# Moving the first quarter of w_out to a float32 load on SyncE, and balancing the first convolution over four tiles

## The chip, the cores and the metric

The kernel runs on one core of one Trainium2 chip. The metric is the device time of one execution in microseconds (us). Before the change it was 718.6 us, the median of five executions (718.43 to 719.05). Where a ratio of two kernels is given, it is the mean time of the one kernel's runs over that of the other's of the same rounds, so it is not quite the ratio of the medians quoted beside it.

## The reference

A causal convolution over seven positions, with one set of softmax weights for each of eight heads, feeds a two-layer network with an ELU between the layers:

```python
w = softmax(weight)                         # 8 heads x 7 taps
out[b, s, h, :] = sum_k w[h, k] * x_pad[b, s + k, h, :]
h = out.reshape(32768, 192) @ w_in          # 192 x 2048
g = where(h > 0, h, exp(min(h, 0)) - 1)
return g @ w_out                            # 2048 x 192
```

## The kernel before

The 32768 tokens are worked off in 32 super-blocks of 1024, and each of them in 16 blocks of 128 hidden columns. For each block and each half of the tokens (a "unit"; there are 1024), TensorE makes h, ACT takes the exponential into E, GpSimd clamps E, VectorE forms gT from E and h, and TensorE multiplies gT by w_out. ACT also reads out the convolution of later super-blocks (csb) and the finished results (osb). A small planner in the kernel fixes the order of the matmuls from estimated landing times (LANDS). All engines work strictly in order.

The first super-block is special. Its convolution runs on x transposed by TensorE, with seven diagonal "tap" matrices, in 64x64 tiles; three of the taps of its first third are made by VectorE:

```python
rows_of = [
    [(0, tap, 0, GS, 0) for tap in range(KSIZE - ON_DVE)]          # ON_DVE = 3
    + [(2, t, GS // 2 * c, GS // 2 * (c + 1), 2 + c) for c in range(2) for t in range(KSIZE)],
    [(1, tap, 0, GS, 1) for tap in range(KSIZE)],
]
```

From the second super-block on, the convolution (the "main conv") uses a band matrix Tm. SyncE makes it by writing wband to DRAM and reading it back in a skewed pattern:

```python
sy.dma_start(xh[:, :], ...)
W(s_tap, 3)
sy.dma_start(<conv_band in DRAM>, wband)       # 288 KB
W(s_band, 16)
sy.dma_start(Tm, band[:, P - 1 : ...])         # 256 KB
... xl; then, when w_in has landed, w_in's upper half by a copy within SBUF
```

GpSimd issues the loads that cast to 16 bits, all before its first clamp:

```python
load_w_in(0); load_w_in(1)                     # six loads
load_w_out(0)                                  # blocks 0 to 3
load_x(1, 0); load_x(1, 1)
load_w_out(1); load_w_out(2)                   # blocks 4 to 7, 8 to 15
load_x(2, 0); load_x(2, 1)
for i, (n, u) in enumerate(units):
    for to_load in x_before.get(i, ()):        # load_x(3, 0) before unit 0
        load_x(*to_load)
    W(s_exp, i + 1)
    g.tensor_scalar(out=E, in0=E, ... ALU.min ... ALU.max)
```

ACT copies the first two parts of w_in into the upper partitions after it has read out the first convolution (att); VectorE copies two more.

## Time and profile before

| | before |
|---|---|
| time, median of 5 | 718.6 us |
| span of the profiled run | 716.9 us |
| TensorE busy; weight loads | 99%; 95% |
| first exponential on ACT | 11.39 us |
| first clamp on GpSimd | 12.88 us |
| first gT on VectorE | 13.54 us |
| Tm landed; first csb on ACT | 18.37; 19.99 us |
| last gT | 706.05 us |

The rows from the first exponential down are start times in the trace, from the start of the span; landings are those of the DMA's semaphore. The steady stretch: 32 units take 21.74 us.

### The profile page before, as it was taken

The page shows a single profiled execution, that of the slowest core. Times are in us where ns is not written, and L with a number is a line of the kernel's source. Part 1 is how long each engine was busy: PE and PEld are TensorE (multiplying, and loading weights), DVE is VectorE, ACT ScalarE, POOL GpSimd, SP SyncE. Part 2 cuts the span into 40 slices and gives each one's busy share as a digit, 9 for nine tenths or more (in the row PEclk, how much of TensorE's full clock was granted, in tenths as well). Part 3 has the DMA queues.
Part 4 walks back from the last instruction along what each step waited for, and adds up shares of the span by engine and source line. Part 5 has one row for each costly group of instructions (what it writes and reads, how often), then busy time and mean ns, then how long its engine had stood idle before and what let it go on. Part 6 is the DMA issues. An engine that isn't in the chain of part 4 may idle for free.

```text
span 716.9 us, 27665 instructions
## 1 busy us (share of the span) xinstructions
PE 711.2 (99%) x11875; PEld 681.8 (95%) x11875; DVE 641.2 (89%) x1048; ACT 677.7 (95%) x1290; POOL 665.1 (93%) x1112
## 2 busy tenths in 40 slices
PE   8999999999999999999999999999999999999998
PEld 4689999999999999999999999999999999999998
DVE  7999889998898998899998989988989988999994
ACT  6999999999999999999999999999999999999994
POOL 9999999999999999999999999999999999999893
PEclk9999999999999999999999999999999999999999
DMA  9635334564443553444553344544445534444212
GB/s 185 97 72 95 66 73 78 94 86 75 79 80 74 94 90 64 78 86 79 87 91 70 72 76 95 87 73 77 84 73 90 94 63 76 88 81 83 62 44 69
DMA packets 132303, 58.80 MB, mean 82 GB/s; under 512 B 98374, under 2 KB 131412, under 8 KB 132180
## 3 DMA queue, kind: packets, MB, share of 16 engines
q0 software_dynamic: 43504, 16.77, 22.4%
q1 hardware_dynamic: 88388, 39.37, 22.2%
q8 instruction: 93, 1.52, 0.9%
q10 hardware_dynamic: 288, 0.88, 0.4%
q14 instruction: 30, 0.25, 0.1%
HBM read 34.63 MB, written 25.46 MB: 84 GB/s over the span
## 4 chain that ended last, share of the span: by engine, by line
PE 96%; POOL 2%; ACT 1%; DVE 0%; issue 0%; DVEq 0%; POOLq 0%
PE H L1052 54%; PE H L1029 37%; PE H L1004 4%; POOL xg L627 1%; ACT E L756 1%; POOL E L710 1%; POOL w_in L647 0%; POOL w_out L658 0%; DVE gT L866 0%; ACT csb L752 0%; POOL owner L675 0%; DVE osb L857 0%; POOL block L685 0%; POOL ident L664 0%; POOL ones L662 0%
## 5 line engine op out<-in xcount | busy, mean ns | idle before, releaser
L866 DVE SCALAR_TENSOR_TENSOR gT<-E,H 128x512 f16<-128x512 f32 x1024 | 631.9, 682 | 63.0 <-POOL E L710 59.0
L1029 PE MATMUL H<-att,w_in 64*128 64x512 bf16 x3072 | 679.9, 376 | 1.3 <-DVE gT L866 1.0
L1052 PE MATMUL H<-w_out,gT 64*128 64x192 f16 x8192 | 680.7, 243 | 0.1
L710 POOL TENSOR_SCALAR E<-E 128x512 f32<-128x512 f32 x1024 | 604.3, 613 | 39.9 <-ACT E L756 33.3
L1052 PEld LDWEIGHTS H<-w_out,gT 64*128 64x128 f16 x8192 | 606.8, 94 | 17.4 <-PE H L1052 1.5
L756 ACT ACTIVATE E<-H 128x512 f32<-128x512 f32 x1024 | 584.9, 600 | 23.9 <-PE H L1029 0.5
L1029 PEld LDWEIGHTS H<-att,w_in 64*128 64x128 bf16 x3072 | 274.9, 93 | 8.1 <-DVE gT L866 3.1
L1004 PE MATMUL H<-xg,Tm 64*128 64x240 bf16 x496 | 90.9, 263 | 0.0
L752 ACT ACTIVATE csb<-H 112x480 bf16<-112x480 f32 x124 | 70.8, 571 | 0.5 <-PE H L1004 0.3
L763 ACT ACTIVATE osb<-H 128x384 f32<-128x384 f32 (+1 forms) x129 | 61.9, 482 | 6.9 <-PE H L1052 6.8
L627 POOL DMA_DIRECT2D xg<-in_x_dram x62 | 54.8, 886 | 0.2 <-issue 0.2
L1004 PEld LDWEIGHTS H<-xg,Tm 64*128 64x128 bf16 x496 | 42.5, 94 | 1.2 <-DVE gT L866 0.3
L857 DVE COPY osb<-H 128x192 f32<-128x192 f32 x1 | 0.4, 357 | 7.3 <-PE H L1052 7.3
L903 PE MATMUL H<-const-bfloat16-1.0 128*128 128x512 bf16 x12 | 4.6, 547 | 0.8 <-PEq L1119 0.8
L903 PEld LDWEIGHTS H<-const-bfloat16-1.0 128*128 128x128 bf16 x12 | 1.4, 126 | 2.7 <-issue 2.5
L647 POOL DMA_DIRECT2D w_in<-in_moe_w_in_dram x6 | 3.6, 611 | 0.0
L732 ACT ACTIVATE xb<-xs 128x512 bf16<-128x512 f32 x2 | 1.1, 622 | 2.4 <-DMA xs<-in_x_dram 2.4
L978 PE MATMUL H<-xT,taps 64*64 64x256 bf16 (+1 forms) x50 | 2.6, 317 | 0.0
L658 POOL DMA_DIRECT2D w_out<-in_moe_w_out_dram x3 | 2.5, 850 | 0.0
L978 PEld LDWEIGHTS H<-xT,taps 64*64 64x64 bf16 x50 | 2.0, 106 | 0.5 <-issue 0.2
L725 ACT ACT_TABLE_LOAD x1 | 1.3, 1283 | 1.2 <-PEq L1119 1.2
L936 PEld LDWEIGHTS H<-ident,xb 64*64 64x64 bf16 x48 | 1.2, 126 | 1.1 <-ACT xb L732 1.1
(44 smaller groups left out, 20.2 us busy)
## 6 DMA issues: line engine op xcount, KB each, us to landing
out_dram<-osb SPq DMA_DIRECT2D x126, 192.0 KB, 2.8
xg<-in_x_dram POOLq DMA_DIRECT2D x61, 240.0 KB, 4.6
xs<-in_x_dram ACTq DMA_DIRECT2D x1, 768.0 KB, 4.6
w_in<-in_moe_w_in_dram POOLq DMA_DIRECT2D x6, 128.0 KB, 4.6
att<-csb SPq DMA_TRANSPOSE x31, 3.9
w_out<-in_moe_w_out_dram POOLq DMA_DIRECT2D x2, 192.0 KB, 8.0
w_out<-in_moe_w_out_dram POOLq DMA_DIRECT2D x1, 384.0 KB, 11.9
w_in<-w_in SPq DMA_DIRECT2D x1, 336.0 KB, 6.7
```

Of the source, the lines that this page charges most:

```text
L627: g.dma_start(xg[0:rows, b, 2 * w0 + gr : 2 * w1 : 2, :], src).then_inc(s_x[b][gr], 16)
L647: g.dma_start(w_in[0:HP, j, c0:c1], bass.AP(tensor=moe_w_in.tensor, offset=8 * j * FF + c0, ap=[[CPH * FF, HEADS], [FF, 8], [1, c1 - c0]], ...
L710: g.tensor_scalar(out=E[:, i % NE, :], in0=E[:, i % NE, :], scalar1=1.0, scalar2=0.0, op0=ALU.min, op1=ALU.max,).then_inc(s_clp)
L752: a.activation(*conv_evac(W, m), ACT.Copy).then_inc(s_ce)
L756: a.activation(E[:, i % NE, :], H[:, bank_of[item], :], ACT.Exp).then_inc(s_exp)
L763: a.activation(*out_evac(W, *item[1:]), ACT.Copy).then_inc(s_oev[item[2]])
L866: v.scalar_tensor_tensor(out=gT[:, s % NG3, q, u, :], in0=E[:, i % NE, :], scalar=1.0, in1=H[:, bank_of[item], :], op0=ALU.subtract, op1=A ...
L903: pe.matmul(H[:, bank, :], nc.const_aps.tensor(1.0, (P, P), BF16), nc.const_aps.tensor(1.0, (P, GS), BF16), start=True, stop=True,)
L978: ins = pe.matmul(H[to, bank_of["d", j] + (j == 2 and c0 > 0), c0:c1], taps[rows, tap, rows], xT[rows, j, HALO - PAD + tap + c0 : HALO - P ...
L1004: ins = pe.matmul(H[:, bank_of["c", m], 256 * q : 256 * q + UC], Tm[rows, h, :], xg[rows, s % NXB, :, CPH * h : CPH * (h + 1)].rearrange(" ...
L1029: ins = pe.matmul(H[:, bank_of[item[:3]], :], w_in[HP * r : HP * (r + 1), j, FC * q : FC * (q + 1)], att[HP * r : HP * (r + 1), s % 2, j, ...
L1052: ins = pe.matmul(acc_of(k, g)[:, D * kb : D * (kb + 1)], gT[HP * rt : HP * (rt + 1), t % NG3, q, g, t0 : t0 + P], w_out[HP * rt : HP * (r ...
```

## The change

Its intent: relieve GpSimd of an issue and a half before its first clamp, and finish the first convolution sooner. The first quarter of w_out (blocks 0 to 3) comes as float32 on SyncE, and VectorE casts it. The other three quarters come in one load. The first convolution is spread over all four tiles, with two taps on VectorE in place of three. ACT's w_in copies move ahead of its att copies. (The diff is cut: the new buffer wo, its semaphore, a memory bank, the planner's lookup and TensorE's wait for the cast are left out.)

```diff
-WOUT = (0, 4, 8, 16)
+WOUT = (0, 4, 16)
-ON_DVE = 3
+ON_DVE = 2
+SPLIT = 352
-LANDS = {... "w_out": (3900.0, 8400.0, 11000.0)}
+LANDS = {... "w_out": (2200.0, 9700.0)}
@@ GpSimd
-            load_w_out(0)
             for gr in range(2):
                 load_x(1, gr)
             load_w_out(1)
-            load_w_out(2)
@@ ACT
+            W(s_w[0], 48)
+            for k in range(2):
+                upper_half(*UPPER[k])
             W(s_first[1], 1)
             a.activation(*first_att(1, 0, GS), ACT.Copy).then_inc(s_fa)
             W(s_first[2], 1)
-            a.activation(*first_att(2, 0, GS // 2), ACT.Copy).then_inc(s_fa)
-            W(s_w[0], 48)
-            for k in range(2):
-                upper_half(*UPPER[k])
+            a.activation(*first_att(2, 0, SPLIT), ACT.Copy).then_inc(s_fa)
@@ VectorE
             (two copies of 64 partitions read the crossed part of att)
+            W(s_w[3], 16)
+            v.tensor_copy(w_out[:, 0 : WOUT[1], :], wo[:, :, :]).then_inc(s_wo)
@@ TensorE
-                        + [(2, t, GS // 2 * c, GS // 2 * (c + 1), 2 + c) for c in range(2) for t in range(KSIZE)],
-                        [(1, tap, 0, GS, 1) for tap in range(KSIZE)],
+                        + [(2, tap, 0, SPLIT, 2) for tap in range(KSIZE)],
+                        [(1, tap, 0, GS, 1) for tap in range(KSIZE)]
+                        + [(2, tap, SPLIT, GS, 3) for tap in range(KSIZE)],
@@ SyncE, between xh and conv_band
+            W(s_xs, 16)
+            sy.dma_start(
+                wo[:, :, :],
+                moe_w_out.rearrange("(q p) d -> p q d", p=FC)[:, 0 : WOUT[1], :],
+            ).then_inc(s_w[3], 16)
```

More of the change, by code (lines that the diff above doesn't have):

```diff
@@ L60 @@
 EARLY_O = (4, 8)
-LANDS = {"x": {1: 7200.0, 2: 14200.0}, "w_in": 10200.0, "w_out": (3900.0, 8400.0, 11000.0)}
+LANDS = {"x": {1: 7200.0, 2: 14200.0}, "w_in": 10200.0, "w_out": (2200.0, 9700.0)}
 DONE_PE, TO_ACT, TO_POOL, TO_DVE, TO_PE = 165.0, 40.0, 85.0, 35.0, 60.0
@@ L266, in o_ready @@
             if k < 2:
-                t = max(t, LANDS["w_out"][next(i for i in range(3) if q1 <= WOUT[i + 1])])
+                t = max(t, LANDS["w_out"][next(i for i in range(2) if q1 <= WOUT[i + 1])])
             if visit == 0:
@@ L456, in bass_lightweight_conv__then__act_elu_kernel @@
         scr = sbuf("scr", [P, 2], FP32)
+        wo = sbuf("wo", [P, WOUT[1], D], FP32)
         H = psum("H", [P, NBANK, GS])
@@ L470, in bass_lightweight_conv__then__act_elu_kernel @@
         s_wb = sema("s_wb")
+        s_wo = sema("s_wo")
         s_xz = sema("s_xz")
@@ L535, in bass_lightweight_conv__then__act_elu_kernel @@
             ("d", 1): (3, 0),
-            ("d", 2): (4, 4),
+            ("d", 2): (4, 5),
         }
@@ L850, in _vector @@
             W(s_first[3], 1)
-            v.tensor_copy(*first_att(2, GS // 2, GS)).then_inc(s_fd)
+            to, at = first_att(2, SPLIT, GS)
+            for g in range(2):
+                v.tensor_copy(
+                    to[HP * g : HP * (g + 1), :], at[HP * (1 - g) : HP * (2 - g), :]
+                ).then_inc(s_fd)
             W(s_w[0], 48)
@@ L976, in _tensor @@
                         for r in range(2):
-                            rows, to = half_of(r), half_of(r ^ (j == 1))
+                            rows, to = half_of(r), half_of(r ^ (which % 2))
                             ins = pe.matmul(
@@ L1048, in _tensor @@
                         W(s_turn[g], turns[k, g])
-                    W(s_w[2 + next(k for k in range(1, 4) if q < WOUT[k])], 16)
+                    if q < WOUT[1]:
+                        W(s_wo, 1)
+                    else:
+                        W(s_w[4], 16)
                     W(s_tt, tt_count(NQ * t + q, g))
```

## The prediction

> **What bounds the kernel now.** I read the busy shares of the page first, then its chain of work that ended last, and then, because the change touches only the start, the same chain and the timelines in the first 26 us. The page says that TensorE fills the run:
>
> ```profile
> PE 711.2 (99%) x11875; PEld 681.8 (95%) x11875; DVE 641.2 (89%) x1048; ACT 677.7 (95%) x1290; POOL 665.1 (93%) x1112
> PE 96%; POOL 2%; ACT 1%; DVE 0%; issue 0%; DVEq 0%; POOLq 0%
> ```
>
> The first line is the busy time of each engine, the second the shares of the chain. The columns that TensorE streams (8192 matmuls of 192, 3072 of 512, 496 of 240, two row halves at a time, at the 2.4 GHz of the granted clock 1.00) come to 680 us of the 716.9 us span. From 65 to 700 us nothing varies: counting the ACT exponentials of the trace, 32 of them go by in 21.74 us, every time. The change touches nothing in there. What it can move is the start: the 13.5 us before the first VectorE result gT, and the ramp after it. The chain there, in order of time (start, length, what):
>
> ```profile
> 2.49 0.73 POOL w_in L647
> 3.22 2.79 POOL w_in L647 x5
> 6.01 0.80 POOL w_out L658
> 6.81 1.72 POOL xg L627 x2
> 8.52 1.64 POOL w_out L658 x2
> 10.16 2.69 POOL xg L627 x3
> 12.88 0.65 POOL E L710
> 13.54 0.70 DVE gT L866
> ```
>
> The reader is to see that GpSimd issues fourteen loads one after the other (six w_in, three w_out, five xg), each 0.6 to 0.9 us of its own time, and that its first clamp (E, L710) starts at 12.88, the moment the last load is issued. Was the clamp's input there earlier? The timelines of ACT and then VectorE (start, length, what, count) say yes:
>
> ```profile
> 9.48 0.60 ACT L742 ACTIVATE att<-H 128x512 bf16<-128x512 f32 x1 [1.13 <-PE H L978]
> 9.98 0.38 ACT L744 ACTIVATE att<-H 128x256 bf16<-128x256 f32 x1
> 10.38 0.93 ACT L734 ACTIVATE w_in<-w_in 64x384 bf16<-64x384 bf16 x2
> 11.39 3.54 ACT L756 ACTIVATE E<-H 128x512 f32<-128x512 f32 x7
> ...
> 8.14 1.54 DVE L842 SCALAR_TENSOR_TENSOR part<-xT,wcol,part 128x512 f32<-128x512 bf16 x2
> 9.71 0.69 DVE L849 TENSOR_TENSOR att<-H,part 128x512 bf16<-128x512 f32 x1
> 10.36 0.42 DVE L851 CAST att<-H 128x256 bf16<-128x256 f32 x1
> 10.81 1.04 DVE L854 COPY w_in<-w_in 64x768 bf16<-64x768 bf16 x2
> 13.54 11.63 DVE L866 SCALAR_TENSOR_TENSOR gT<-E,H 128x512 f16<-128x512 f32 x19 [1.69 <-POOL E L710]
> ```
>
> The first exponential ends 0.60 us after 11.39, at 11.99, so the clamp waits 0.89 us for GpSimd alone. VectorE then idles 1.69 us and runs 19 steps with no gap: between 13.5 and 25.2 it is the bound of the ramp, at 0.598 us from start to start.
>
> **What the Trainium skill says.** "DMA: Bandwidth & Descriptors", section "Issuing engines are not separate DMA queues": loads from SyncE, ACT and GpSimd run on the same 16 DMA engines, and another issuer saves only its own issue time. The trace agrees on the issue time: 0.86 us of GpSimd for the first w_out load, against 0.36 us of SyncE for the conv_band copy. So a transfer gains nothing by moving, GpSimd does. The same page, "SWDGE vs HWDGE vs iDMA": a cast during the load is for GpSimd's path only; that is why w_out from SyncE must come as float32 and be cast. All casting loads of the trace are indeed GpSimd's. "VectorE: DVE Perf Modes", section "Why PSUM operands drop a tier": a one-source float32 copy within SBUF goes at two elements a cycle, from PSUM at one. The trace agrees: the 128x512 cast of xs in SBUF and the 128x256 cast of att out of PSUM both took 425 ns. "TensorEngine Tiling (Array Packing)", section "Key Properties": different tiles run in parallel. The trace agrees for the first conv: its first four matmuls started within 0.01 us.
>
> **The change, part by part.**
> - GpSimd: one w_out issue goes to SyncE (0.86 us off), two become one. The 4-row-block load took 0.78, the 8-block one 0.92; I estimate 0.98 for 12, so 0.72 off. Last issue done at 12.85 - 1.58 = 11.27, before any clamp can start.
> - First conv: the diagonal tile pair streamed 4x512 + 14x256 = 5632 columns, the crossed pair 3584. Now 5x512 + 7x352 = 5024 against 3584 + 7x160 = 4704. The end moves by 608 / 2.4 = 0.25 us, from 10.32 to 10.07. VectorE loses one 0.75 us tap (L842) and its add (L849) starts when five taps are through: 7.73 + 5x0.215 + 0.2, near 9.1, instead of 9.71. It ends near 9.8.
> - ACT: the two w_in copies (0.93) move ahead of att. They need the third w_in load, which landed at 8.55 in the trace; so 8.6 to 9.5, att second third 9.5 to 10.1, then 352 columns, 10.1 to 10.6. VectorE's part of att, two copies of 160 columns out of PSUM at 425 - 96/0.96 = 325 ns each, ends near 10.6 too. The first matmul group then completes near 11.1 and the first exponential starts at about 11.15 instead of 11.39.
> - Clamp: 11.15 + 0.6 = 11.8 instead of 12.88, so 1.05 to 1.1 us earlier; gT could start at 12.45.
> - VectorE cast: 128x768 in SBUF, 425 + 128/0.96 = 558 ns. After the att copies and the w_in copies (1.04) VectorE is free at 11.65; with the cast by 12.2, just inside the hole that it had.
> - Sum at the first gT: 13.54 to about 12.5, 1.0 us on the path. Since VectorE bounds the ramp, all of it could reach the end. 718.6 - 1.0 = 717.6.
>
> **What may eat it.** SyncE's transfers are slow in this stretch (KB, us from issue to landing):
>
> ```profile
> w_in<-w_in SPq DMA_DIRECT2D x1, 336.0 KB, 6.7
> conv_band<-wband SPq DMA_DIRECT2D x1, 288.0 KB, 6.0
> Tm<-conv_band SPq DMA_DIRECT2D x1, 256.0 KB, 5.5
> ```
>
> The new 384 KB load is issued at 5.45, when xs has landed. By these rows it takes 6 to 7.4 us and lands between 11.5 and 12.9.
>
> **Rivals.**
> 1. The cast is the new wait. VectorE works in order; if the load lands at 12.9, the cast ends at 13.5 and the first gT stands where it stood. For it: the three rows above. Against it: from 4 to 10 us the DMA share was 0.91, against 1.58 from 12 to 16, so there was room. Time then 718.4 to 718.6.
> 2. The band for the main conv comes later. conv_band queues behind the new load on SyncE. In the trace it landed at 12.9, Tm at 18.4, and the first main conv matmul ran at 19.16, only 0.8 us later. If the ramp is 1.0 us earlier and Tm 0.6 us later, TensorE and then ACT (its first csb at 19.99, in fixed order) wait for Tm, and 0.1 to 0.4 us of the gain are left. For it: the order on SyncE. Against it: 384 KB have left GpSimd's queue. Time 718.2 to 718.5.
> 3. w_out for blocks 4 to 7, formerly there at 17.1, comes with the rest. The trace had the rest at 21.2; I estimate 19 to 20.5, as 384 KB less stand before it. The new order of the matmuls asks for it 9.7 us after the first h matmul, at about 20. A stall of up to 1 us of TensorE is possible: 718.2 to 719.2. Against it: TensorE had 0.6 us of each 2 us unused from 24 to 30, by the columns that it streamed.
> 4. Everything passes, and the reordered ramp packs better: 717.2.
>
> **Range and chances.** Full passage 717.6, the rivals 718.2 to 718.6, about evenly likely: 718.0. The low end is the fourth rival, the high end the third with half its stall, with the spread of the runs before (0.6 us) in mind: 717.2 to 718.8. Two per cent is 14 us, more than the whole start; nothing here reaches it, and the steady stretch keeps its order, so 0.99 for the same.
>
> **What would show it.** Right: GpSimd's first clamp near 11.8, first gT near 12.5, the exponentials of 65 to 700 us again 32 per 21.74 us and all shifted by the same 0.2 to 1.0 us. The cast about 0.56 us. Rival 1: VectorE idle before the cast, waiting for wo. Rival 2: TensorE or ACT idle at 18 to 20 with Tm landing after 18.5. Rival 3: TensorE idle before a w_out matmul near 20. I am wrong if the period of the steady stretch changes at all, since then the order of the matmuls there is not what I take it for.

## The result, and the profile after

The changed kernel takes 720.06 us, the median of five executions (719.30 to 720.56), against 718.6 before: a ratio of 1.002, 95% interval 1.0006 to 1.0033. It is slower by some 1.5 us, and outside the range of the prediction, though by the measure of 2% the two are the same, as it gave with 0.99. The slowdown does not hang on the clock: the three executions at clock 1.000 took 719.30, 719.89 and 720.22 us, the two at 0.998 took 720.06 and 720.56. The profiled execution is its fastest, 719.30 us, so the trace shows about half of the loss.

The page of the changed kernel, engines' busy time and the shares of the chain that ended last:

```profile
PE 711.6 (99%) x11877; PEld 681.1 (95%) x11877; DVE 641.7 (89%) x1049; ACT 677.1 (94%) x1290; POOL 662.4 (92%) x1110
PE 96%; DMA 2%; POOL 0%; DVE 0%; ACT 0%; issue 0%; DVEq 0%
```

TensorE is as busy as before. But where the chain had 2% of GpSimd, it now has 2% of DMA. The chain in order of time (start, length, what) tells which:

```profile
6.97 7.73 DMA conv_band<-wband
...
14.72 5.28 DMA Tm<-conv_band
...
20.05 0.26 PE H L1013
...
20.90 0.58 ACT csb L753
```

It runs over the two legs of the band matrix, conv_band and Tm, to the first matmul of the main conv (L1013) and to ACT's first csb. That was at 19.99 before. The timelines of ACT, GpSimd and VectorE (start, length, what, count, idle before and its end) show what else came later:

```profile
9.97 0.94 ACT L735 ACTIVATE w_in<-w_in 64x384 bf16<-64x384 bf16 x2 [1.56 <-DMA w_in<-in_moe_w_in_dram]
10.93 0.60 ACT L746 ACTIVATE att<-H 128x512 bf16<-128x512 f32 x1
...
12.36 3.54 ACT L757 ACTIVATE E<-H 128x512 f32<-128x512 f32 x7 [0.48 <-PE H L1038]
...
8.72 2.64 POOL L630 DMA_DIRECT2D xg<-in_x_dram  x3
13.05 8.41 POOL L711 TENSOR_SCALAR E<-E 128x512 f32<-128x512 f32 x14 [1.69 <-ACT E L757]
...
13.16 0.91 DVE L861 CAST w_out<-wo 128x768 f16<-128x768 f32 x1 [1.28 <-DMA wo<-in_moe_w_out_dram]
13.99 8.44 DVE L873 SCALAR_TENSOR_TENSOR gT<-E,H 128x512 f16<-128x512 f32 x14
```

GpSimd has issued its loads at 11.36, 1.5 us earlier than before, as intended; its first clamp then waits for ACT. ACT waits for w_in before it reads att: its third load landed at 9.95 in place of 8.55. VectorE waits for the float32 load, which lands at 13.14, casts for 0.91 us, and starts its first gT at 13.99, against 13.54. The issues by tile (KB, us to landing) show the new load and the copy behind it on SyncE, which took 6.0 us before:

```profile
wo<-in_moe_w_out_dram SPq DMA_DIRECT2D x1, 384.0 KB, 7.8
...
conv_band<-wband SPq DMA_DIRECT2D x1, 288.0 KB, 7.7
```

After the ramp, 32 units again take 21.74 us. Unit 64's gT starts 1.02 us later than before, the last one 0.77 us later; a little is given back in every fourth stretch.

### The profile page after: what moved, and what is told of

Same layout as the page of the kernel before. It is cut to its first block, busy times and chain, and to the rows that moved or that the text cites. A ratio compares the mean times of both kernels' runs of the same rounds, so it can differ in the third digit from the quotient of the medians.

```text
span 717.4 us, 27669 instructions
## 1 busy us (share of the span) xinstructions
PE 711.6 (99%) x11877; PEld 681.1 (95%) x11877; DVE 641.7 (89%) x1049; ACT 677.1 (94%) x1290; POOL 662.4 (92%) x1110
## 4 chain that ended last, share of the span: by engine, by line
PE 96%; DMA 2%; POOL 0%; DVE 0%; ACT 0%; issue 0%; DVEq 0%
PE H L1064 54%; PE H L1038 37%; PE H L1013 4%; DMA conv_band<-wband 1%; DMA Tm<-conv_band 1%; PE H L910 0%; POOL E L711 0%; ACT E L757 0%; ACT csb L753 0%; POOL xg L630 0%; DVE gT L873 0%; DVE xbh L819 0%; DVE taps L808 0%; DVE xb L815 0%; DVE osb L864 0%
## 5 line engine op out<-in xcount | busy, mean ns | idle before, releaser
L1013 PE MATMUL H<-xg,Tm 64*128 64x240 bf16 x496 | 90.9, 263 | 0.5 <-DMA Tm<-conv_band 0.2
L1013 PEld LDWEIGHTS H<-xg,Tm 64*128 64x128 bf16 x496 | 42.6, 94 | 2.4 <-ACT csb L753 1.0
L735 ACT ACTIVATE w_in<-w_in 64x384 bf16<-64x384 bf16 x3 | 1.5, 516 | 1.6 <-DMA w_in<-in_moe_w_in_dram 1.6
L987 PE MATMUL H<-xT,taps 64*64 64x512 bf16 (+2 forms) x52 | 2.3, 319 | 0.0
```

The lines of the kernel that those rows point to most:

```text
L987: ins = pe.matmul(H[to, bank_of["d", j] + (j == 2 and c0 > 0), c0:c1], taps[rows, tap, rows], xT[rows, j, HALO - PAD + tap + c0 : HALO - P ...
L1013: ins = pe.matmul(H[:, bank_of["c", m], 256 * q : 256 * q + UC], Tm[rows, h, :], xg[rows, s % NXB, :, CPH * h : CPH * (h + 1)].rearrange(" ...
```

## The experiments

Three theories stand against each other. **CAST**: the load lands late, VectorE works in order, and its cast holds up the first gT. **BAND**: conv_band stands behind the new load on SyncE's queue, so Tm and the main conv are late. **ACT**: the copies moved ahead of att wait for w_in. A fourth came up on the way, **MERGE**: blocks 4 to 7 of w_out come only with the whole rest. All runs were timed in five rounds; the kernel before ran beside each group, at 718.39, 718.41 and 718.34 us (medians).

| run | median us | ratio to before, 95% interval | first gT | Tm landed | first csb | last gT |
|---|---|---|---|---|---|---|
| before | 718.6 | | 13.54 | 18.37 | 19.99 | 706.05 |
| changed kernel | 720.06 | 1.0020 (1.0006 to 1.0033) | 13.99 | 20.00 | 20.90 | 706.82 |
| a_actback | 720.00 | 1.0021 (1.0009 to 1.0034) | 14.35 | 20.44 | 21.34 | 707.27 |
| a_bandfirst | 723.40 | 1.0068 (1.0054 to 1.0082) | 17.47 | 18.91 | 26.12 | 712.09 |
| a_poolfirst | 718.78 | 1.0003 (0.9991 to 1.0016) | 12.88 | 18.89 | 19.79 | 706.72 |
| a_pool_act | 718.98 | 1.0005 (0.9993 to 1.0018) | 12.79 | 19.15 | 20.05 | 706.52 |
| c_conv | 718.27 | 0.9997 (0.9985 to 1.0010) | 13.52 | 18.41 | 19.97 | 705.82 |
| c_move | 719.00 | 1.0008 (0.9996 to 1.0021) | 12.81 | 18.66 | 19.55 | 706.39 |
| c_early | 718.30 | 1.0003 (0.9989 to 1.0017) | 13.14 | 19.08 | 19.98 | 705.67 |
| b_wo | 719.73 | 1.0025 (1.0012 to 1.0037) | 14.77 | 20.55 | 23.48 | 709.18 |
| d_bandlate | 722.19 | 1.0053 (1.0040 to 1.0065) | 13.59 | 21.20 | 22.10 | 707.84 |
| d_castlate | 720.41 | 1.0029 (1.0017 to 1.0042) | 14.54 | 19.20 | 20.97 | 706.84 |
| d_actfirst | 718.73 | 1.0008 (0.9994 to 1.0021) | 13.24 | 18.89 | 19.79 | 705.48 |
| e_actcast | 718.31 | 0.9999 (0.9986 to 1.0011) | 13.42 | 18.95 | 19.87 | 705.70 |

The last four columns are from each kernel's one profiled execution, in us from its start. That execution can lie well off the median (b_wo's took 722.05 us, d_bandlate's 720.57), so its times are compared with its own, not with the medians.

### First group: undo one part of the change

**a_actback** puts ACT's order back.

```diff
             for j in range(1, 3):
                 ...transposed...
-            W(s_w[0], 48)
-            for k in range(2):
-                upper_half(*UPPER[k])
             ...first_att(1), first_att(2)...
+            W(s_w[0], 48)
+            for k in range(2):
+                upper_half(*UPPER[k])
```

> The changed kernel with ACT's two w_in copies put back behind its att copies. Theory CAST (the float32 load lands at 13.1 and VectorE casts before its first gT) and theory BAND (Tm lands at 20.0, 1.6 later than before) say that this alone brings nothing: the first exponential starts near 11.5 instead of 12.36, but the first gT stays near 14.0 and the time near 720.0. Theory ACT (the copies wait for a w_in load that now lands 1.4 later and hold att up) says that the 1 us lost at the first exponential was the loss at the end: 719.0.

The first exponential came back to 11.55, and nothing was gained: 720.00 us. Theory ACT falls as the one cause. The profiled execution took 720.00 us and shows, in passing, a more typical run of this pair than the changed kernel's own profile: its float32 load landed at 13.77, Tm at 20.44, and its last gT is 1.2 us later than before.

**a_bandfirst** issues conv_band before the float32 load.

```diff
@@ SyncE
-            W(s_xs, 16)
-            sy.dma_start(wo, ...).then_inc(s_w[3], 16)
             W(s_tap, 3)
             sy.dma_start(<conv_band>, wband).then_inc(s_band, 16)
+            W(s_xs, 16)
+            sy.dma_start(wo, ...).then_inc(s_w[3], 16)
```

> The changed kernel with the conv_band copy issued before the float32 w_out load on SyncE. Theory BAND: Tm is back near 18.5 to 19 and the kernel is back at 718.7 to 719.0. Theory CAST: the float32 load now lands near 14.5 to 15 instead of 13.1, the first gT moves from 14.0 to about 15.3, and the time goes up by 0.3 to 1 us, to 720.5.

Tm is back at 18.91, and yet this is the slowest of all, 723.40 us; the float32 load now landed at 16.55. The waits from 8 to 32 us (who, for whom, us in all, times, longest):

```profile
DVE w_out L861 <- DMA wo<-in_moe_w_out_dram: 4.7, 1, 4.7
...
PE H L1064 <- DVE gT L873: 3.7, 1, 3.7
```

VectorE stood 4.7 us before its cast. So the cast can hold up everything behind it. That the time grew by more than was expected has a second part, which the view by stretches shows (us, busy time of TensorE, its weight loads, VectorE, ACT and GpSimd, granted clock, DMA):

```profile
14.00:18.10 4.10, 0.49 (x5) 0.00 (x0) 1.53 (x3) 2.43 (x5) 3.13 (x6) 1.00 1.44 231
18.10:24.90 6.80, 6.63 (x46) 3.71 (x47) 6.20 (x11) 3.16 (x6) 3.03 (x5) 0.50 1.28 194
24.90:32.00 7.10, 6.89 (x78) 3.99 (x75) 5.66 (x9) 6.89 (x14) 5.41 (x11) 1.00 0.01 3
```

After TensorE had stood for 3.7 us, its granted clock was 0.5 from 18.11 to 24.93, and a matmul of 512 columns took some 631 ns in place of 376. That is up to 3.4 us of TensorE's work (an estimate: half of 6.83). In b_wo the same drop, 15.84 to 22.67, followed a pause of 2.0 us; the pauses of 1.8 us (d_bandlate) and 1.4 us (d_castlate) were followed by none in their profiles. That the pause causes the drop is not tested by a run of its own. Two transfers on one queue, each of them urgent: whichever comes second is late.

**a_poolfirst** takes the SyncE load and the cast away; GpSimd loads the first quarter as before. **a_pool_act** puts ACT's order back besides.

```diff
@@ a_poolfirst
-            sy.dma_start(wo, ...).then_inc(s_w[3], 16)              # SyncE
-            v.tensor_copy(w_out[:, 0 : WOUT[1], :], wo[:, :, :]).then_inc(s_wo)
+            load_w_out(0)                                           # GpSimd, behind load_w_in(1)
-                        W(s_wo, 1)                                  # TensorE
+                        W(s_w[3], 16)
```

> The changed kernel without the SyncE load and without VectorE's cast: GpSimd loads the first quarter with its cast where it did before, and the rest in one. Conv and ACT's order stay as changed. If the SyncE load is the one cause of all three delays, then the third w_in load lands near 8.6 again, the first exponential starts near 11.2, GpSimd has issued its last load at 12.15, the first gT starts at 12.8 (before: 13.54) and Tm lands at 18.4: 718.0, faster than before by 0.6. If ACT's order is a cause of its own, the first exponential stays late and the time is 718.7 or more.

> As the run before (no SyncE load), and ACT's two w_in copies back behind att. If ACT's order costs only where w_in lands late, this is the same as the run before within 0.2 us, 718.0; if the order is a cause of its own, this one is faster by 0.5 or more.

The two are alike within noise (718.78 and 718.98), so ACT's order is no cause of its own. The loss against before is gone within the interval, so the SyncE load was the cause of it. The gain that I expected did not come, though the first gT started at 12.88 and 12.79, as foretold. The chain of a_poolfirst between 12 and 30 us says why:

```profile
8.43 13.43 DMA w_out<-in_moe_w_out_dram
...
21.99 0.24 PE H L1063
```

The one big load of w_out landed at 21.86, and TensorE's first matmul with block 4 waited for it. Before, those blocks had landed at 17.08, with their own load. The lead at unit 12 (20.07 against 20.72) had turned into a lag at unit 18 (25.58 against 24.50). In the changed kernel itself this wait was hidden: the rest landed at 20.05, and the first matmul with block 4 ran at 22.41, held up by other things.

### Second group: parts alone, and another place for the load

**c_conv** is the kernel before with the balanced conv alone (its lines on TensorE, VectorE and ACT, without the cast and without moving ACT's copies).

> The kernel before with the balanced first conv alone (four tiles, two taps on VectorE); GpSimd loads w_out in three pieces as before, ACT's order as before. The first exponential starts near 11.45, as in the last run of the call before, but GpSimd issues until 12.85, so the first gT stays at 13.5. Theory MERGE (with the SyncE load gone, the loss was the 1.0 us wait for blocks 4 to 7, which came with the one big load at 21.9): no such wait here, 718.4 to 718.6, the time of before. If the loss of the last two runs was of the conv itself, this one is at 718.9.

It is as expected: 718.27 against 718.41 us, the same within the interval, with no wait for w_out. The conv does no harm, and its gain is hidden behind GpSimd's issues. Against a_pool_act, which differs by the merged load and its landing times, it also shows what merging cost: its last gT is 0.7 us earlier although its first is 0.7 us later. MERGE stands.

**c_move** adds one edit: `X3_AT = (0, 48)` becomes `(16, 48)`, so that GpSimd is free 0.85 us sooner.

> The same with one more edit: GpSimd issues the first half of the x load of super-block 3 before its 17th clamp and not before its first. It has issued its loads by 12.0, the first gT starts at 12.8, blocks 4 to 7 of w_out land near 17. Theory MERGE: no wait there, and the lead of 0.7 us lasts until the main conv, which needs Tm at 18.4 to 19.2; half of it is left after that: 718.1. Theory BAND in its strong form (whatever happens before, the ramp restarts when Tm lands): 718.5, no gain.

The first gT started at 12.81 and the lead of 0.7 us lasted to unit 12, both as expected. Then the moved issue itself stood between two clamps: from the gT of unit 14 to that of unit 16 it took 2.08 us in place of 1.20. At the end nothing was left (719.00). Here the issue of 0.9 us cost as much at its new place.

**c_early** keeps the float32 load but lets ACT issue it at 1.2 us, right behind xs (the load of the first x); the rest of w_out comes in two loads, and ACT's copies stand behind att (hunks not shown). The planner keeps the changed kernel's early landing time for the first quarter (2200).

```diff
@@ ACT
             a.dma_start(xs[:, :, :], ...).then_inc(s_xs, 16)
+            a.dma_start(wo[:, :, :], <first quarter of w_out>).then_inc(s_w[3], 16)
@@ SyncE
-            W(s_xs, 16)
-            sy.dma_start(wo, ...).then_inc(s_w[3], 16)
```

> The float32 load of the first quarter again, but issued by ACT right behind its xs load, at 1.2 instead of 5.4, and not on SyncE; w_out's rest in two loads; ACT's copies behind att; conv as changed. If what hurt was the place on SyncE's queue before conv_band and the late issue, then it lands before 10, the cast (0.55 us, no clamp running) hides, the first gT starts at 12.8, Tm lands before 19 and the time is 718.0 to 718.3. If what hurt was the transfer itself, w_in and conv_band come later by 1 us or more here too: 719.5.

The load landed at 7.31. The timeline of VectorE:

```profile
12.07 0.56 DVE L866 CAST w_out<-wo 128x768 f16<-128x768 f32 x1
13.14 1.29 DVE L878 SCALAR_TENSOR_TENSOR gT<-E,H 128x512 f16<-128x512 f32 x2 [0.50 <-POOL E L712]
```

Now the cast fits into the hole before the first gT, which is 0.40 us earlier than before. The same bytes, early and on a queue with nothing urgent behind them, cost nothing: 718.30 us (one execution of the five took 719.58). So neither the transfer itself nor the planner's landing time is to blame, although the third w_in load landed at 9.78 here. It is no gain either: Tm landed at 19.08, and the first csb came at 19.98, where it was.

**b_wo** is the reverse: the kernel before plus the SyncE load and the cast, and the planner's landing time for this quarter (2200 for 3900); c_early has shown that landing time to be harmless.

> The kernel before with the SyncE load and VectorE's cast alone; the rest of w_out in two loads, conv and ACT's order as before. If the SyncE load is the one cause: the float32 load lands near 13.2 to 13.8, the cast takes 0.4 to 0.9, the first gT starts near 14.2, Tm lands at 20.0 to 20.4, and the time is 719.5 to 720.0, as of the whole change. If it takes ACT's order or the one big load besides, 718.8.

719.73 us, 1.3 over before: this one part makes the loss of the whole change. Its profile fell on its slowest execution (722.05), with the float32 load landing at 14.17, Tm at 20.55 and the clock at 0.5 for 6.83 us. The loss is there without that: the three executions at clock 1.000 took 719.38 to 719.73.

### Third group: one wait added to a kernel that has neither

The parts so far move two transfers at once. c_early has both of them in time, so one wait can be added to it at a time, without a byte more.

**d_bandlate**: SyncE waits for the third w_in load before conv_band.

```diff
+            W(s_w[0], 48)
             W(s_tap, 3)
             sy.dma_start(<conv_band>, wband).then_inc(s_band, 16)
```

> The early load from ACT's queue (718.3), with one wait added: SyncE issues conv_band only when the third w_in load has landed, near 9.8 instead of 7.1. No byte is added. Theory BAND: Tm lands 1 us or more later, at 20.0 or beyond, with the first gT unchanged near 13.1; ACT's first csb waits for it, near 21, and the end is 0.8 to 1.2 us later: 719.3. If the band is not on the path, 718.3.

Tm landed 2.1 us later than in c_early, more than the 1 us foreseen, at 21.20. ACT's timeline from 17 to 24 us:

```profile
22.10 0.57 ACT L758 ACTIVATE csb<-H 112x480 bf16<-112x480 f32 x1 [2.13 <-PE H L1018]
```

The last gT is 2.17 us later than in c_early. BAND is shown: Tm's landing goes through to the end one for one in this execution, which took 720.57 us. The median, 722.19, is far over the 719.3 foreseen. The profiled execution is the only one at clock 1.000; the other four show 0.995 to 0.998 and took 722.13 to 723.23. So the further 1.6 to 2.7 us go with a lower clock; no profile shows where in those executions it fell.

**d_castlate**: VectorE waits for conv_band before its cast.

```diff
+            W(s_band, 16)
             W(s_w[3], 16)
             v.tensor_copy(w_out[:, 0 : WOUT[1], :], wo[:, :, :]).then_inc(s_wo)
```

> The early load from ACT's queue, with one wait added: VectorE does its cast of w_out only when conv_band has landed, near 13.6, as if the load had come then. Theory CAST: the cast runs at 13.6 to 14.4, beside a clamp, the first gT starts near 14.4 instead of 13.1; half or all of the 1.3 us reaches the end: 719.0 to 719.6. If the wait is swallowed before the main conv, which waits for Tm at 19.1 anyway, 718.4.

VectorE's timeline from 9 to 16 us:

```profile
13.97 0.65 DVE L867 CAST w_out<-wo 128x768 f16<-128x768 f32 x1 [1.92 <-DMA conv_band<-wband]
14.54 1.87 DVE L879 SCALAR_TENSOR_TENSOR gT<-E,H 128x512 f16<-128x512 f32 x3
```

The first gT is 1.40 us later than in c_early and the last one 1.17 us, with Tm in time (19.20). The time, 720.41, is over the range given (719.11, 720.41 and 720.42 at clock 1.000; 720.18 and 721.81 at 0.998). CAST is shown too, by itself.

**d_actfirst**: ACT's copies ahead of att again.

> The early load from ACT's queue, with ACT's two w_in copies before its att copies as in the changed kernel. The third w_in load landed at 9.8 with the early load, so att is held up: first exponential near 12.2 instead of 11.73, first gT 13.6 instead of 13.1. Theory ACT: 0.3 to 0.5 us of that at the end, 718.7. If the main conv's wait for Tm at 19.1 swallows it, 718.3.

The third w_in load landed at 9.49, the first gT moved by 0.10 us only, and the last gT was even 0.19 us earlier. The times spread from 717.96 to 719.56, so a few tenths stay undecided; a loss of the size looked for is not there.

**e_actcast** gives the cast to ACT, between xT and att.

> The early load from ACT's queue, with the cast of w_out done by ACT in its idle time between its xT and its att copies (8.5 to 9.6) and not by VectorE. The cast takes 0.8 to 0.9 us and hides there; the first gT starts at 12.95 to 13.0, when the first clamp ends, instead of 13.14. At most 0.2 us: 718.1 to 718.3. If ACT's cast runs past 9.6 and holds att up, 718.5 or more.

The cast took 0.83 us there, and ended before att's input was there. In this execution everything on ACT from its xT copies on had started 0.4 us later, so the first gT (13.42) says nothing. 718.31 against 718.34 us: the same. No version beats the kernel before beyond the noise.

### What the table says as a whole

In 12 of its 14 rows the first csb is, within 0.03 us, the later of two times: the first gT plus 6.45, or Tm's landing plus 0.90. Before, the first term gave 19.99 and the second 19.27; in the changed kernel they give 20.44 and 20.90. The two exceptions, a_bandfirst and b_wo, are the two with the clock at 0.5 in between, after waits of TensorE for VectorE of 3.7 and 2.0 us; they miss the rule by 2.2 and 2.0 us. d_castlate, with such a wait of 1.4 us at full clock, keeps it, so the wait alone is not what it misses. And the last gT follows the first csb by 685.7 to 686.1 us in all rows but three, by 686.5 to 686.9 in these: a_poolfirst and a_pool_act, with their wait for block 4, and c_move, with the moved issue. So the whole start acts through one point, the first read-out of the main conv. This is a fit to these runs, not a law.

## Why the prediction was wrong

It stood at 718.0 us (717.2 to 718.8); measured were 720.06. By its own steps:

- **GpSimd's issues**: right. Foretold to end at 11.27, they ended at 11.36. (The merged load took 1.10 us of issue where 0.98 was estimated; and one of the old issues had taken 1.03, above the stated 0.6 to 0.9.)
- **The first conv**: right. It was to end at 10.07 and ended at 9.97; VectorE's add was to start near 9.1 (its sum gives 9.0) and started at 9.03.
- **ACT's copies and the first exponential**: wrong. The step "they need the third w_in load, which landed at 8.55 in the trace" took one landing in one trace of the old kernel for that of the new. It landed at 9.95, and the first exponential came at 12.36, not 11.15. It cost nothing at the end (a_actback), since the cast held up gT longer anyway. Whether the float32 load made it late stays open: in the five profiled kernels without that load it landed at 8.47 to 10.09.
- **The cast**: mis-sized. It was 558 ns in the working and 910 in the run. Its start was the load's landing at 13.14, just past the stated 11.5 to 12.9 (the sum at the first gT had let it start at 11.65, near the early end), while a clamp was running (13.05 to 13.66); it ended 0.41 us after that clamp. Started before the clamp, in c_early, it took 560.
- **"The first gT stands where it stood"** (rival 1) and **"0.1 to 0.4 us of the gain are left"** (rival 2): this is the step that failed. Both rivals were rightly named, and both came true. But each was allowed to eat the gain and no more. A new transfer that an engine must wait for has no reason to land just when the old chain ended. The load put the first gT 0.45 us behind, and Tm was 1.63 us later where I had put 0.6. The lateness of Tm was the longer of the two: 0.91 us at the first csb, 0.77 at the last gT of this trace. The rest of the median's 1.5 us lies in executions that were not profiled. That transfers landed still later there is likely from a_actback's profile, but is only argued; two of the four had a lower mean clock (0.998) besides. That a late transfer could also cost clock was in no rival; a_bandfirst and b_wo show it as a sequence.
- **"All of it could reach the end"**: wrong as well, even without any rival. By the fit above, Tm's landing at 18.37 left 0.72 us of room at the first csb, so at most that much of the 1.0 us could ever have passed.
- **Rival 3**, the late blocks of w_out: the landing was right (20.05, in the stated 19 to 20.5). It was not the bound in the changed kernel, but it was the next one, as a_poolfirst showed. It is why taking the SyncE load away gave no gain.
- **The steady stretch**: right, 21.74 us for 32 units.

The argument "there was room", from a DMA share of 0.91 between 4 and 10 us, misled me. A mean share says that the engines could take more bytes. It doesn't say when the bytes of one queue get their turn beside a full one.

## What to carry to other kernels

An engine's issue time can be bought back by moving a load to another queue, but the queue it goes to may hold something more urgent: look at what stands behind it, and at how long that queue's transfers take in just this stretch. When a wait is replaced by another, size the new one by itself and never cap its cost at the gain. A wait at the start can also cost more than its length: in two profiles here TensorE's clock was halved for 6.83 us after one. And before counting a gain at the end of a ramp, find the first point where the ramp meets a chain that the change doesn't shorten; here it was a landing with 0.7 us of room.

## What the Trainium skill lacked or had wrong

- "DMA: Bandwidth & Descriptors", section "Specifications": it gives some 0.6 us to the first byte for transfers issued by SyncE or ACT. Beside a full GpSimd queue, the first packet of conv_band left 3.1 us after its issue ended (7.23 to 10.30, kernel before), and that of the float32 load 2.4 us after (5.78 to 8.20, changed kernel). The transfers took 5.3 to 7.8 us for 256 to 384 KB. The page has no figure for this case.
- Same page, section "Issuing engines are not separate DMA queues": it says that another issuing engine saves only issue time. The same 384 KB landed at 7.31 when ACT issued them at 1.2 us and at 13.14 when SyncE did at 5.4, and on SyncE they pushed conv_band's landing from 12.90 to 14.71. When a load is issued, and what stands behind it on its queue, decided the sign of this change; this section doesn't say so. "Queues, rings and completion order" on the same page has the order (the descriptors of one ring are consumed in ring order), but no figure of what standing behind another transfer costs.
- "SBUF — State Buffer", section "SBUF: two separate sides": it says that a VectorE copy in a two-port mode and a GpSimd operation exclude each other for their whole length. The traces agree: in the five where the cast started during a clamp (changed kernel, a_actback, a_bandfirst, b_wo, d_castlate) it took 631 to 973 ns and ended 0.41 to 0.42 us after that clamp; in the three where it started first it took 560. In the changed kernel the clamp behind it took 907 ns in place of 608. Nothing was wrong there; "VectorE: DVE Perf Modes", section "Why PSUM operands drop a tier", which I used for the 558 ns, doesn't mention it.
